# Attention ahead of two expert layers: scaled queries, a negated maximum, and the order of VectorE's step

## The chip, the cores and the metric

One core of a Trainium2 chip runs the whole program. The metric is the device time of one execution in microseconds; "before" is the median of three runs, 1357.63 us (1355.26 to 1357.83). Every profile shown is of one execution.

## The reference, cut to what matters

Two batches, 8 heads, 576 positions, head size 64, all in fp32. A score counts only if it is within tau (0.02) of its row's largest; the rest gets no weight. The attention's output goes through a layer of 8 experts and then one of 4.

```python
scale = 1.0 / np.sqrt(q.shape[-1])                       # 0.125
scores = scale * np.matmul(q, k.transpose(0, 1, 3, 2))
thresh = np.max(scores, axis=-1, keepdims=True) - tau
scores = np.where(scores >= thresh, scores, -1000000000.0)
scores = scores - np.max(scores, axis=-1, keepdims=True)
attn = np.exp(scores)
attn = attn / (np.sum(attn, axis=-1, keepdims=True) + 1e-09)
return np.matmul(attn, v).astype(np.float32)
```

## The kernel before, in words

The program has two parts. In the first, about 250 us, attention runs, and PE does matmuls of the first experts in between (the "fill"). In the second the remaining experts run, with PE busy throughout.

**Units.** Attention is cut into 72 units of 128 query rows against all 576 keys. A unit's scores are two halves of 288 columns in one PSUM tile `sc`, of which there are two. The units come in three groups: 16 "exact" ones (batch 0, queries 0 to 255; weights and values multiplied in plain fp32), 20 (batch 0, the other 320 queries) and 36 (batch 1). Precision beyond fp32r comes from splitting an operand into an fp32r part and the fp32r rest. The first four units (`ws`, the first pair of heads) multiply unsplit queries and keys (L261); the other 68 use queries split by `prep` (L270). A head pair's two leftovers of 64 queries share one unit, whose operands come from `qz`.

**A step.** `step` (L389) issues, in program order, work on up to seven units that stand at different places of the pipeline. Each engine executes its own instructions in that order; semaphores hold an instruction until its inputs are there. With t the step:
- `turn` of unit t-2: PE transposes the normalized weights into `et` (L306), which has one buffer, and `er` (L308).
- `mask` of unit t (VectorE, L288): weights times (score >= threshold), with the row sum as a by-product.
- `top` of unit t+1 (VectorE, L275): the row maximum, read from PSUM.
- `guard` of t (L292), `line` of t+1 (L279: maximum times -0.125, the exponential's bias; L280: the threshold), `norm` of t (L296: reciprocal; L298: GpSimd multiplies the weights by it).
- `hi` of t-2 (ScalarE, L313): the transposed weights as fp32r. `out`: copies of finished products.
- up to three pieces of fill, four matmuls each, and while the exact units run a weight tile split by `cook` (ScalarE cast L96, then GpSimd L98 or VectorE L100).
- `exp` of t+1 (ScalarE, L284): exponential of 0.125 x score + bias, both from per-partition tiles (`esc`, `st`).
- `lo` of t-2 (VectorE, L323, L326): the rest of the transposed weights. The next `turn` needs `et` back from it.
- `scores` of t+2 (PE): needs the buffer that `mask` of t read last.
- deferred subtractions (`later`: L370, L359, L470), the products with the values (L348, L350), more fill, `late` splits.
- work that `plan` (L183) has put at this step for a head that is still to come: keys (`pk`: ScalarE cast L71, GpSimd L76), queries (`pq`: ScalarE cast L239, GpSimd subtraction L240 and, for a leftover, L243), values (`pv`). 22 heads have a `pq`; it comes at least one step ahead of the first scores that use it.

Loads of keys, queries and values go through SP's queue, in order, into two (values: three) buffers, and wait until the split of the tile's former content has read it.

**Scalars.** `on` is 1 if tau is not negative (L527), and then turned into 0 or a huge number (L530); `esc` is 0.125 times it; `lin` holds -0.125 and 8 tau plus `on` (L527 to L531). With unscaled scores the threshold is maximum - 8 tau.

Of the kernel before, what the change touches and what calls it, by code (L numbers as in the profile page):

```python
# [11 lines left out]
AF = mybir.ActivationFunctionType  # L12
ALU = mybir.AluOpType
AX = mybir.AxisListType
# [9 lines left out]
HS = S // 2  # L24
# [5 lines left out]
def attention_two_moe_kernel(ctx, tc, qP, kP, qT, kT, vp, tau, wg, w1, w1s, w2, dp, m2w1s, m2w2, out):  # L30
    nc = tc.nc
    V, A, G, T = nc.vector, nc.scalar, nc.gpsimd, nc.tensor

    def f(ap):
        return ap.bitcast(F32)

    def pool(stack, name, bufs=1, **kw):
        return stack.enter_context(tc.tile_pool(name=name, bufs=bufs, **kw))
# [15 lines left out]
    tau_sb = cp.tile([P, 1], F32, name="tau_sb")  # L54
    warm = cp.tile([P, 1], F32, name="warm")
    A.activation(warm, ones[:, 0:1], AF.Exp)
    esc = cp.tile([P, 1], F32, name="esc")
    lin = cp.tile([P, 2], F32, name="lin")
    on = cp.tile([P, 1], F32, name="on")
# [9 lines left out]
    def split(eh, el, hi, lo, src):  # L69
        if eh is A:  # L70
            A.copy(hi, src)  # L71
        elif eh is V:
            V.tensor_copy(hi, src)
        else:
            G.tensor_scalar(hi, src, 1.0, 1.0, op0=ALU.mult, op1=ALU.mult)
        el.tensor_tensor(lo, src, f(hi), op=ALU.subtract)  # L76
# [34 lines left out]
    class Attention:  # L111
# [117 lines left out]
        def prep(self, hd):  # L229
            pl = self.pl  # L230

            def pk():
                hd["kh"] = pl.tile([P, S], F32R, tag="kh", name="kh", bufs=2)
                hd["kl"] = pl.tile([P, S], F32R, tag="kl", name="kl", bufs=2)
                split(A, G, hd["kh"], hd["kl"], hd["k"])

            def pq():
                qs = hd["qs"] = pl.tile([P, hd["n"]], F32R, tag="qs", name="qs", bufs=2)
                A.copy(qs, hd["q"])  # L239
                G.tensor_tensor(qs[D:], hd["q"][D:], f(qs[D:]), op=ALU.subtract)  # L240
                if hd["rem"]:
                    c, z = hd["rem"]
                    G.tensor_scalar(hd["z"][:, z:z + D], f(qs[:, c:c + D]), 1.0, 1.0, op0=ALU.mult, op1=ALU.mult)  # L243
                self.lq -= 1

            def pv():
                hd["vs"] = pl.tile([P, 5, 2, D], F32R, tag="vhl", name="vhl", bufs=2)
                split(A, G, hd["vs"][:, :, 0, :], hd["vs"][:, :, 1, :], hd["v"])
                self.lv -= 1

            return (pk, pq) if hd["exact"] else (pk, pq, pv)
# [20 lines left out]

        def top(self, u):
            st = u["st"] = self.pl.tile([P, 8], F32, tag="st", name="st", bufs=6)
            V.tensor_reduce(st[:, 0:1], u["sc"][:, :, :HS], axis=AX.XY, op=ALU.max)  # L275

        def line(self, u):
            st = u["st"]
            V.tensor_scalar(st[:, 1:2], st[:, 0:1], lin[:, 0:1], None, op0=ALU.mult)  # L279
            V.tensor_scalar(st[:, 2:3], st[:, 0:1], lin[:, 1:2], None, op0=ALU.subtract)  # L280

        def exp(self, u):
            ex = u["ex"] = self.pl.tile([P, 2, HS], F32, tag="ex", name="ex", bufs=4)
            A.activation(ex, u["sc"][:, :, :HS], AF.Exp, bias=u["st"][:, 1:2], scale=esc)  # L284

        def mask(self, u):
            st, ex = u["st"], u["ex"]
# [101 lines left out]
        def step(self, fill, side):  # L389

            us, t = self.units, self.t
            un = lambda i: us[i] if 0 <= i < len(us) else None
            self.load()
            nxt, a, d, x, c, z, y = (un(t + i) for i in (2, 1, 0, -2, -3, -4, -5))
            if x:
                self.turn(x)
            if d:
                self.mask(d)
            if a:
                self.top(a)  # L400
            if d:
                self.guard(d)
            if a:
                self.line(a)
            if d:
                self.norm(d)
            for part, u in ((2, y), (1, z), (0, c)):
                for g in u["mix"] if u else ():
                    if g["head"]["exact"]:
                        self.mix(g, part)  # L410
            if x:
                self.hi(x)
            for u, late in ((z, False), (y, True)):
                for g in u["mix"] if u else ():
                    if late == (g["head"]["exact"] and g["head"]["h"] < H - 1):
                        self.out(g)
            fill(0, bool(c and c["mix"]))
            if a:
                self.exp(a)
            if x:  # L420
                self.lo(x)
            if nxt:
                self.scores(nxt)
            self.run(self.later)
            for g in c["mix"] if c else ():
                if not g["head"]["exact"]:
                    self.mix(g, 0)
            fill(1, bool(c and c["mix"] or z and z["mix"]))
            self.run(self.late)
            for w in self.work.pop(t, ()):  # L430
                w()
            side()
            self.t += 1
            return self.t < len(us) + 5
# [74 lines left out]
    with ExitStack() as att:  # L509
        ap = pool(att, "attn", side="right")  # L510
        ps_s = pool(att, "ps_s", 2, space=PSUM)
        ps_t = pool(att, "ps_t", 1, space=PSUM)
        ps_r = pool(att, "ps_r", 1, space=PSUM)
        banks.pool = ps = pool(att, "ps_m", 2, space=PSUM)
        at = Attention(ap, ps_s, ps_t, ps_r, ps)
        for p in range(H // 2):
            at.add_pair(0, p, 0, 256, True, p == 0)
        nA0 = len(at.units)
        for p in range(H // 2):
            at.add_pair(0, p, 256, 320, False)  # L520
        nA1 = len(at.units)
        for p in range(H // 2):
            at.add_pair(1, p, 0, S, False)
        at.plan()
        room = [2 * FT]
        at.load()
        V.tensor_scalar(on, tau_sb, 0.0, None, op0=ALU.is_ge)  # L527
        V.tensor_scalar(esc, on, 0.125, None, op0=ALU.mult)
        V.tensor_scalar(lin[:, 0:1], on, -0.125, None, op0=ALU.mult)
        V.tensor_scalar(on, on, -BIG, BIG, op0=ALU.mult, op1=ALU.add)  # L530
        V.scalar_tensor_tensor(lin[:, 1:2], tau_sb, 8.0, on, op0=ALU.mult, op1=ALU.add)  # L531

        def side():
            if at.t >= -1:
                fetch(2)
            if at.t >= nA0 - 3 and raws and room[0] and (at.t < nA1 or room[0] > 2 or at.t % 2):
                room[0] -= 1
                cook()
            if at.t == 20:
                nc.sync.dma_start(wg_sb, wg)  # L540
                nc.sync.dma_start(dp_sb, dp)
            if at.t == 24:
                split(V, V, wg2[:, :, :E1], wg2[:, :, E1:], wg_sb)

        def free(n):
            room[0] += n

        X0, X1 = Expert(0), Expert(1)
        near, far = ((0, 0), (1, P)), ((2, 32), (3, 32 + P))
        todo = [(nA0 + 3, expert_fill(hp, X0, 0, 256, near, acc, None, 0, at.later, keep)),  # L550
                (nA1 + 3, expert_fill(hp, X0, 256, 320, far, acc, tail0[0], 0, at.later, free)),
                (nA1 + 3, expert_fill(hp, X1, 0, 256, near, y1, None, 0, at.later, keep)),
                (nA1 + 3, expert_fill(hp, X1, 256, 320, far, y1, tail0[1], 0, at.later, keep))]

        left, spent = [0], [0]

        def pull(n, end=True):

            for i in range(n):
                if not todo or at.t <= todo[0][0] or (left[0] == 1 and not end):  # L560
                    return i
                left[0] = next(todo[0][1], -1)
                if left[0] < 0:
                    todo.pop(0)
                if left[0] <= 0:
                    left[0] = 0
                    return i + 1
            return n

        def fill(phase, busy):  # L570
            if phase == 0:
                if 0 <= at.t < nA0 - 3:
                    room[0] -= 1
                    cook(None if at.t % 2 else at.later)
                spent[0] = pull(3)
            elif left[0] or not busy:
                pull(max((RA1 if at.t < nA1 + 3 else RA2) - spent[0], 0), True)

        while at.step(fill, side):
            pass  # L580
        at.flush()
        while left[0]:
            pull(1)
        at.flush()
        while raws:
            cook()
            fetch(2)
# [492 lines left out]
```

## Time and profile before

| | |
|---|---|
| median of 3 runs | 1357.63 us (1355.26 to 1357.83) |
| profiled execution: its span, first to last instruction | 1353.7 us |
| profiled execution: its own time | not printed; the three runs lie 1.6 to 4.1 us above the span |
| PE busy | 1320.6 us, 98% |
| VectorE (DVE) busy | 679.6 us, 50% |
| ScalarE (ACT) busy | 562.3 us, 42% |
| GpSimd (POOL) busy | 688.6 us, 51% |
| first and last mask (L288) start | 7.9 and 238.5 us |

Busy shares are means over two very different parts: VectorE is full in attention and half idle behind it. PE's matmuls are pipelined, and a busy PE includes time in which one matmul's end waits; how far PE is from its limit is better read from its waits. "Idle before" and a releaser in brackets say which instruction ended the idle time ahead of an instruction on its engine.

### The profile page before, as it was taken

The page shows a single profiled execution, that of the slowest core. Times are in us where ns is not written, and L with a number is a line of the kernel's source. Part 1 is how long each engine was busy: PE and PEld are TensorE (multiplying, and loading weights), DVE is VectorE, ACT ScalarE, POOL GpSimd, SP SyncE. Part 2 cuts the span into 40 slices and gives each one's busy share as a digit, 9 for nine tenths or more (in the row PEclk, how much of TensorE's full clock was granted, in tenths as well). Part 3 has the DMA queues.
Part 4 walks back from the last instruction along what each step waited for, and adds up shares of the span by engine and source line. Part 5 has one row for each costly group of instructions (what it writes and reads, how often), then busy time and mean ns, then how long its engine had stood idle before and what let it go on. Part 6 is the DMA issues. An engine that isn't in the chain of part 4 may idle for free.

```text
span 1353.7 us, 21670 instructions
## 1 busy us (share of the span) xinstructions
PE 1320.6 (98%) x8089; PEld 1181.8 (87%) x8089; DVE 679.6 (50%) x1600; ACT 562.3 (42%) x1291; POOL 688.6 (51%) x830
## 2 busy tenths in 40 slices
PE   7998999999999999999999999999899999999998
PEld 4588999899888989899898989989789889898987
DVE  6899999365853433434343343434433434343343
ACT  6877777322542423323242332325433334242331
POOL 5866976441774345345434533544963554354330
PEclk9999999999999999999999999999999999999999
DMA  5522330100221111111011111101111101110001
GB/s 173 173 85 72 93 96 26 32 24 24 91 66 39 55 47 40 48 40 62 24 55 47 40 48 40 63 24 56 37 34 55 48 24 56 47 60 27 32 8 63
DMA packets 42058, 73.63 MB, mean 54 GB/s; under 512 B 5088, under 2 KB 10336, under 8 KB 41952
## 3 DMA queue, kind: packets, MB, share of 16 engines
q1 hardware_dynamic: 41664, 71.96, 16.8%
q8 instruction: 64, 1.05, 0.3%
q14 instruction: 42, 0.34, 0.1%
q10 hardware_dynamic: 288, 0.28, 0.1%
HBM read 69.86 MB, written 2.36 MB: 53 GB/s over the span
## 4 chain that ended last, share of the span: by engine, by line
PE 83%; DVE 8%; POOL 4%; ACT 3%; issue 2%; DMA 1%; POOLq 0%; ACTq 0%; DVEq 0%
PE mm L997 37%; PE mm L887 32%; PE mm L489 5%; PE mm L461 3%; DVE ex L288 2%; DVE st L275 1%; PE sc L270 1%; PE et L306 1%; ACT ex L284 1%; PE pv L350 1%; PE pv L341 1%; PE pv L348 1%; POOL wl L76 1%; DVE etl L323 1%; DVE xy L772 0%
## 5 line engine op out<-in xcount | busy, mean ns | idle before, releaser
L997 PE MATMUL mm<-wh,hs 128*128 128x512 f32 x1344 | 436.7, 398 | 3.7 <-DVE hs L863 3.7
L76 POOL TENSOR_TENSOR wl<-raw,wh 128x512 fp32r<-128x512 f32 x154 | 199.1, 1304 | 328.4 <-ACT wh L71 326.5
L997 PEld LDWEIGHTS mm<-wh,hs 128*128 128x128 f32 x1344 | 253.0, 188 | 66.3 <-DVE hs L863 10.1
L1005 DVE SCALAR_TENSOR_TENSOR acc<-mm,p,acc 128x512 f32<-128x512 f32 x181 | 135.9, 751 | 308.1 <-PE mm L997 308.1
L997 PE MATMUL mm<-wl,hs 128*128 128x512 f32 x672 | 264.7, 394 | 0.0
L892 ACT COPY s<-mm 128x288 f32<-128x288 f32 x84 | 33.6, 401 | 453.5 <-PE mm L887 453.5
L863 DVE SCALAR_TENSOR_TENSOR hs<-mm,hs 128x288 fp32r<-128x288 f32 x252 | 114.8, 456 | 104.0 <-ACT hs L862 103.7
L997 PEld LDWEIGHTS mm<-wl,hs 128*128 128x128 f32 x672 | 127.0, 189 | 27.3
L887 PE MATMUL mm<-xh,wl 128*128 128x288 f32 x672 | 144.3, 296 | 2.6 <-ACT w L892 1.4
L887 PE MATMUL mm<-xl,wh 128*128 128x288 f32 x672 | 143.8, 295 | 0.0
L887 PE MATMUL mm<-xh,wh 128*128 128x288 f32 x672 | 143.8, 295 | 0.0
L862 ACT ACTIVATE hs<-mm 128x288 fp32r<-128x288 f32 x252 | 104.2, 414 | 71.8 <-DVE mm L914 66.6
L76 POOL TENSOR_TENSOR wl<-ws,wh 128x512 fp32r<-128x512 f32 x88 | 114.5, 1305 | 36.6 <-ACT wh L71 26.9
L887 PEld LDWEIGHTS mm<-xh,wl 128*128 128x128 f32 x672 | 110.0, 188 | 7.3 <-ACT w L892 1.9
L887 PEld LDWEIGHTS mm<-xh,wh 128*128 128x128 f32 x672 | 108.1, 188 | 0.0
L887 PE MATMUL mm<-xth,wl 128*128 128x288 f32 x504 | 107.9, 295 | 0.0
L887 PEld LDWEIGHTS mm<-xl,wh 128*128 128x128 f32 x672 | 107.9, 188 | 0.0
L887 PE MATMUL mm<-xth,wh 128*128 128x288 f32 x504 | 107.7, 295 | 0.0
L887 PE MATMUL mm<-xtl,wh 128*128 128x288 f32 x504 | 107.7, 295 | 0.0
L869 POOL TENSOR_SCALAR ht<-hs 128x128 fp32r<-128x128 f32 x168 | 49.2, 298 | 112.9 <-ACT hs L862 97.8
L71 ACT CAST wh<-raw 128x512 fp32r<-128x512 f32 x154 | 95.7, 624 | 13.3 <-PE mm L887 10.4
L625 POOL TENSOR_TENSOR ws<-raw 128x512 f32<-128x512 f32 x44 | 57.7, 1311 | 54.6 <-DMA raw<-in_w1s 32.5
(169 smaller groups left out, 2412.0 us busy)
## 6 DMA issues: line engine op xcount, KB each, us to landing
raw<-in_w SPq DMA_DIRECT2D x88, 256.0 KB, 3.0
raw<-in_w1s SPq DMA_DIRECT2D x56, 256.0 KB, 2.8
raw<-in_m2w1s SPq DMA_DIRECT2D x32, 256.0 KB, 2.7
raw<-in_m2w SPq DMA_DIRECT2D x32, 256.0 KB, 2.8
kr<-in_kT SPq DMA_DIRECT2D x22, 288.0 KB, 2.9
vr<-in_vp SPq DMA_DIRECT2D x24, 160.0 KB, 2.3
qr<-in_qT SPq DMA_DIRECT2D x8, 288.0 KB, 2.8
out_y<-acc SPq DMA_DIRECT2D x8, 256.0 KB, 2.0
```

The source lines that it names most:

```text
L71: A.copy(hi, src)
L76: el.tensor_tensor(lo, src, f(hi), op=ALU.subtract)
L461: T.matmul(ph[:, :n], lhsT=a[:, kt * P:(kt + 1) * P], rhs=x[:, kt, n0:n0 + n], start=i == 0 and kt == 0, stop=i == 2 and kt == KT - 1)
L489: T.matmul(py[:, :256], lhsT=x, rhs=a[:, c0:c0 + 256], start=i == 0, stop=i == 3 * FT - 1)
L625: G.tensor_tensor(s, a, b, op=op)
L862: A.activation(hh, src, AF.Relu)
L863: V.scalar_tensor_tensor(hl, src, 0.0, f(hh), op0=ALU.max, op1=ALU.subtract)
L869: G.tensor_scalar(tail[j][:, :, q:q + 32], f(side[s][j][:, :, 2 * P:]), 1.0, 1.0, op0=ALU.mult, op1=ALU.mult)
L887: T.matmul(m, lhsT=w[:, (2 * g + kt) * P:(2 * g + kt + 1) * P], rhs=operand(u, kt, lo), start=first and j == 0, stop=j == len(ops) - 1, sk ...
L892: A.copy(z[name], m)
L997: T.matmul(py, lhsT=hs[x][:, k, o:o + P], rhs=w, start=n == 0, stop=n == 3 * HF - 1)
L1005: V.scalar_tensor_tensor(acc[t], py, s, acc[t], op0=ALU.mult, op1=ALU.add)
```

## The change

Four edits, all in attention:
- `pq` multiplies the queries by `esc` in place, with a ScalarE activation (Copy with a scale from a tile), ahead of the cast. The scores of 68 units are then already scaled.
- `top` writes the negated maximum for these units, `exp` takes it as its bias directly and has no scale tile; the four unsplit units keep the old form.
- `line` is one instruction for these units: maximum - (tau + `on`), formed from the negated maximum; `on` gets tau added once at the start.
- In the step, VectorE's order becomes maximum (t+1), mask (t), line (t+1), guard (t), reciprocal (t); it was mask, maximum, guard, line, reciprocal.

```diff
             def pq():
                 qs = hd["qs"] = pl.tile([P, hd["n"]], F32R, tag="qs", name="qs", bufs=2)
+                A.activation(hd["q"], hd["q"], AF.Copy, scale=esc)
                 A.copy(qs, hd["q"])
                 G.tensor_tensor(qs[D:], hd["q"][D:], f(qs[D:]), op=ALU.subtract)
...
         def top(self, u):
             st = u["st"] = self.pl.tile([P, 8], F32, tag="st", name="st", bufs=6)
-            V.tensor_reduce(st[:, 0:1], u["sc"][:, :, :HS], axis=AX.XY, op=ALU.max)
+            V.tensor_reduce(st[:, 0:1], u["sc"][:, :, :HS], axis=AX.XY, op=ALU.max, negate=not u["q"][0][0]["ws"])
 
         def line(self, u):
             st = u["st"]
+            if not u["q"][0][0]["ws"]:
+                V.tensor_scalar(st[:, 2:3], st[:, 0:1], -1.0, on, op0=ALU.mult, op1=ALU.subtract)
+                return
             V.tensor_scalar(st[:, 1:2], st[:, 0:1], lin[:, 0:1], None, op0=ALU.mult)
             V.tensor_scalar(st[:, 2:3], st[:, 0:1], lin[:, 1:2], None, op0=ALU.subtract)
 
         def exp(self, u):
             ex = u["ex"] = self.pl.tile([P, 2, HS], F32, tag="ex", name="ex", bufs=4)
-            A.activation(ex, u["sc"][:, :, :HS], AF.Exp, bias=u["st"][:, 1:2], scale=esc)
+            if u["q"][0][0]["ws"]:
+                A.activation(ex, u["sc"][:, :, :HS], AF.Exp, bias=u["st"][:, 1:2], scale=esc)
+            else:
+                A.activation(ex, u["sc"][:, :, :HS], AF.Exp, bias=u["st"][:, 0:1])
...
             if x:
                 self.turn(x)
+            if a:
+                self.top(a)
             if d:
                 self.mask(d)
             if a:
-                self.top(a)
+                self.line(a)
             if d:
                 self.guard(d)
-            if a:
-                self.line(a)
-            if d:
                 self.norm(d)
...
         V.scalar_tensor_tensor(lin[:, 1:2], tau_sb, 8.0, on, op0=ALU.mult, op1=ALU.add)
+        V.tensor_tensor(on, tau_sb, on, op=ALU.add)
```

## Rows read from the trace of the kernel before

**Rows 1.** The head of the page.
```profile
span 1353.7 us, 21670 instructions
```

**Rows 2.** Stretches: busy us of PE, PEld, DVE, ACT, POOL; granted clock, DMA share, GB/s.
```profile
31.94:66.00 34.06, 32.13 (x169) 19.11 (x167) 27.17 (x92) 28.10 (x54) 29.66 (x32) 1.00 0.58 173
66.00:120.84 54.84, 51.33 (x404) 49.41 (x403) 51.22 (x156) 39.63 (x79) 34.69 (x43) 1.00 0.28 83
120.84:180.39 59.55, 55.09 (x410) 52.29 (x409) 55.62 (x168) 44.77 (x86) 48.90 (x79) 1.00 0.29 90
180.39:239.50 59.11, 57.59 (x462) 56.00 (x461) 55.16 (x171) 44.54 (x87) 39.18 (x43) 1.00 0.16 48
```

**Rows 3.** Chain that ended last, in order of time: start us, us, what.
```profile
27.02 0.73 PE sc L270 x4
...
39.10 0.84 ACT ex L284
39.96 0.82 DVE ex L288 x2
40.78 0.67 DVE st L275
```

**Rows 4.** Waits (us, times, longest): VectorE 5-66, 66-240; PE 66-240 (two); PE 5-66.
```profile
DVE ex L288 <- ACT ex L284: 10.0, 13, 1.7
...
DVE ex L288 <- ACT ex L284: 5.0, 18, 0.6
...
PE et L306 <- DVE etl L323: 6.3, 9, 1.0
PE sc L270 <- DVE ex L288: 2.0, 3, 1.0
...
PE sc L270 <- POOL qs L240: 2.8, 2, 2.4
```

**Rows 5.** Groups by form, 0 to 250 us: busy us, mean ns, idle before.
```profile
L284 ACT ACTIVATE ex<-sc,st,esc 128x576 f32<-128x576 f32 x72 | 59.9, 832 | 16.5 <-DVE st L279 14.5 <-POOL ex L298 0.5 <-POOL wl L98 0.5
...
L275 DVE TENSOR_REDUCE st<-sc 128x1 f32<-128x576 f32 x72 | 54.2, 752 | 0.8 <-PE sc L261 0.8
...
L279 DVE TENSOR_SCALAR st<-st,lin 128x1 f32<-128x1 f32 x72 | 15.4, 214 | 0.0
...
L280 DVE TENSOR_SCALAR st<-st,lin 128x1 f32<-128x1 f32 x72 | 14.7, 204 | 0.0
```

**Rows 6.** Timeline of VectorE's small instructions in one step: start us, us, instruction.
```profile
88.66 0.14 DVE L292 TENSOR_SCALAR st<-st 128x1 f32<-128x1 f32 x1
88.78 0.21 DVE L279 TENSOR_SCALAR st<-st,lin 128x1 f32<-128x1 f32 x1
88.91 0.20 DVE L280 TENSOR_SCALAR st<-st,lin 128x1 f32<-128x1 f32 x1
```

**Rows 7.** Timeline of the first units, 0 to 34 us.
```profile
3.49 4.35 PE L261 MATMUL sc<-kr,qr 64*128 64x288 f32 x8 [3.49 <-DMA qr<-in_qP]
...
5.96 0.76 DVE L275 TENSOR_REDUCE st<-sc 128x1 f32<-128x576 f32 x1 [0.79 <-PE sc L261]
...
8.91 2.25 PE L261 MATMUL sc<-kr,qr 64*128 64x288 f32 x4 [1.06 <-DVE ex L288]
...
15.51 0.85 PE L270 MATMUL sc<-kh,qs 128*128 128x288 f32 x2 [0.39 <-POOL qs L240]
...
16.16 0.68 PE L270 MATMUL sc<-kl,qs 128*128 128x288 f32 x2
...
18.85 0.74 POOL L298 TENSOR_SCALAR ex<-ex,st 128x576 f32<-128x576 f32 x1 [2.55 <-DVE st L296]
...
23.06 0.54 PE L270 MATMUL sc<-kh,qs 128*128 128x288 f32 x2 [2.38 <-POOL qs L240]
```

**Rows 8.** The query cast's line: duration ns min/median/max, first and last start.
```profile
L239 ACT CAST qs<-qr x22: 392/458/679, 13.2 to 216.5; 128x320 fp32r<-128x320 f32 x8, 128x576 fp32r<-128x576 f32 x8, 128x256 fp32r<-128x256 f32 x6
```

**Rows 9.** L270's idle time before its matmuls and weight loads, by releaser: us, times.
```profile
  DVE ex L288: 9.8, 15
```

## The prediction

> **What bounds the kernel now.** I read the span first [rows 1], then the attention part in stretches [rows 2], because the diff touches nothing after it. Behind about 250 us the order of the instructions stays as it is and PE is the engine that is always busy, so a microsecond won or lost in attention should show whole at the end. The three runs have a median of 1357.63 us. The profiled execution has a span of 1353.7 us; its own time is not printed beside it, so 3.9 us stand around the span if it was a median run and 1.6 us if it was the fastest (1355.26). I work out a difference from its rows and set it against the median.
>
> In the stretches behind 66 us VectorE is 93% busy (51.22 + 55.62 + 55.16 of 173.5 us), ScalarE 74%, GpSimd 71%. PE reads 95%, but its spans are modelled, and what it idles is better seen in its waits. A step there takes about 3.3 us ((239.5 - 66) / 53 units). In the stretch before, 31.94 to 66, no engine is full: DVE 80%, ACT 83%, POOL 87%. There the chain of waits goes round a ring [rows 3]: exponential 0.84, mask 0.82, maximum 0.67 us, then the guard and the first threshold instruction, and the next exponential. With 0.12 + 0.21 us for these two and small handoffs it is 2.7 us, one unit per round, each waiting for the one before.
>
> The waits say the same [rows 4]: the mask waited for the exponential 10.0 us in 13 places up to 66 us and 5.0 us in 18 places behind it. PE's longest wait behind 66 us is 6.3 us in nine places, for the low halves that VectorE subtracts last in a step (L323). So late in attention VectorE's time is the limit in some steps, PE's own work in the others.
>
> **The change, part by part.**
> *One small instruction less.* For 68 of the 72 units (all but the four on unsplit scores) L279 disappears; L280 becomes an instruction with two scalar operands of the same size, priced the same, 0.204 us. L279 lasts 0.214 us [rows 5], but the next starts 0.13 us after it [rows 6], so VectorE wins 0.13 a unit: 68 x 0.13 = 8.8 us of busy time, 6.9 of them behind 66 us (53 units). The exponential's bias is now the maximum itself, which takes guard and L279 out of the ring too.
> *Negation inside the reduction.* No row shows it. Nothing excludes a cost up to one small instruction, 0.14 us by the guard of rows 6, and nothing suggests a gain. I take 0.752 us as before; the upper end is 72 x 0.14 = 10 us. The single extra addition at the start (as small) lies before the first maximum, where VectorE waits for scores anyway.
> *Order: maximum, mask, threshold, guard, reciprocal.* The maximum no longer queues behind a mask that waits for an exponential, so the ring is cut: VectorE reduces the next unit while ScalarE exponentiates. What replaces it is another loop. There are two score buffers; the mask of unit t frees the one for the scores of t+2, and the maximum of t+2 now stands in front of the mask of t+1. So the new ring is mask 0.82, scores 0.73 (rows 3, at 27.02), maximum 0.67 to 0.75, and handoffs: 2.4 us. In the middle stretch that is 0.3 us a unit for some 12 units, 3.6 us. POOL's 29.66 of 34.06 us caps it at 4.4, so I take 2.5; the ends are 0 and 4.4. Moved with it are only VectorE instructions: no DMA is issued there and no queue of SP or POOL is passed. But the reciprocal comes a maximum later (0.67 us), and POOL's normalization with it. PE transposes that unit two steps later, so about three microseconds cover it; without that cover PE would lose up to 0.67 a unit.
> *Behind 66 us* the offer is 6.9 us of small instructions and 5.0 of mask waits. PE can only take what it stalls, and the part that hangs on VectorE is 6.3 + 2.0 us in rows 4. I take 6.0; the ends are 0, if PE's own work fills the steps, and 8.3.
> *The start, where the new ring costs.* Scores of the first units are slow [rows 7]: 2.25 us a unit for L261, 1.33 for the first L270 (15.51 to 16.84). Walk: maximum 1 at 7.9, mask 0 to 9.4, scores 2 to 11.8, maximum 2 to 12.6, mask 1 to 13.4, scores 3 to 15.7, maximum 3 to 16.5, mask 2 to 17.3, scores 4 to 18.7, maximum 4 to 19.5, mask 3 to 20.3, normalization 3 at 20.7. Before it was 18.85, and POOL had waited 2.55 us for it, so POOL starts its full stretch 1.9 us late, and the scores at 23.06, which wait for POOL's split of the queries, come that much later: +1.9 us.
> *The queries scaled in place.* 22 more ScalarE instructions stand ahead of the cast that L239 does. No row shows a Copy with a pointer scale. From below it is the cast of the same tile, 0.392 to 0.679 us, median 0.458 [rows 8], 22 x some 0.5 = 11 us; from above the exponential, 0.832 with two pointer operands on the widest tile [rows 5], 1.24 times as much, 14 us. I take the cast, since both are plain passes from SBUF. ScalarE idles a quarter of the late stretches, and the split is made a step or more before its scores, so this lies beside other work but for two places where PE waited for POOL's share (2.8 us in rows 4, two times): 2 x 0.4 = 0.8 us. If the cover is gone it is the full 11 to 14.
> *The exponential without a scale operand.* It lies between 0.832 (as now) and the widest cast, 0.679. I take 0.832; at the other end ScalarE wins 68 x 0.15 = 10 us, nearly all of it idle time.
> The Trainium skill, "ScalarE: Activation LUTs", section "What ACT_TABLE_LOAD costs", says that each pointer operand of an ACTIVATE adds about 93 ns. That speaks against the scaled copy (22 x 0.093 = 2.0 us more) and for the exponential (68 x 0.093 = 6.3 us less); no row of this trace has the same tile with one and with two, and by the page the sum would be about 1 us better, 0.093 for each of some dozen units of the middle stretch.
>
> **Sum:** -2.5 - 6.0 + 1.9 + 0.8 = -5.8, taken as -5.6: 1357.6 - 5.6 = **1352.0 us**.
>
> **Rivals.**
> *PE is the bound.* PE would be late by its own work in nearly all steps behind 66 us, VectorE's waits would move elsewhere, and only 2.5 of the middle would stand against 2.7 of start and copies: 1357.8, no change. For it: PE 95% busy, 57.59 of 59.11 in the last stretch. Against: nine stalls for VectorE of 0.7 us each.
> *The score buffer becomes the wait (slower).* PE waited for a mask in 15 places, 9.8 us in sum, before the scores of L270 [rows 9]. If each mask comes a maximum later, each of these grows by 0.67: 10 us, and with the start 1.9 it is 11.9 against 8.8 of instructions saved: +3.1, 1360.7 us. It decides if PE's added wait is over 0.13 us a unit on average, which is what the dropped instruction brings. Against it: in the late steps PE has fill matmuls ahead of the scores, and the maximum starts earlier than before.
> *All stalls go.* The middle gives 4.4, behind 66 us all 8.3 go, the scaled copies are hidden and the start costs 0.7: -12.0, 1345.6 us.
> That the change does not do what it says (a bias that still waits for the threshold instruction) would show in the waits and give the PE-bound time.
>
> **Numbers.** Forecast 0.55 (own range 1347 to 1355), PE bound 0.20, score buffer 0.13, all stalls gone 0.12. A measurement of this kernel tells about 0.2% from no change (2.7 us). Faster is 0.55 + 0.12 = 0.67, same 0.20, slower 0.13. The range leaves out about half of the fastest and half of the slowest case: 1345 to 1360.5.
>
> **What would show it.** Right: the mask's wait for the exponential falls from 15 us to under 3; L279 has 4 instances; the chain of 31.94 to 66 has no three-piece ring; stalls for L323 fall from 6.3 us to about 2; POOL's normalization 3 comes near 20.7; total VectorE busy time falls by about 9 us. Wrong: the maximum waits for scores, or the scores for the mask, in most steps; POOL's query split is waited for in more than a few places; or attention ends earlier but what follows gives it back, which my sum excludes.

## The result, and the profile after

The changed kernel takes 1363.4 us (1362.74 to 1365.22, four runs), 1.0057 of the kernel before, 95% interval 1.0045 to 1.0069: 7.7 us slower, where 5.6 us less were forecast. The time lies outside the range, on the other side. The two medians as printed, 1363.4 and 1357.63, are only 5.8 us apart, because the kernel before was run just three times here (a fourth execution of it took 2225.16 us and is left out); 79 later runs of it, in the four sessions of the experiments, have medians of 1355.6 to 1355.93, 7.5 to 7.8 below the changed kernel. Executions of one kernel differ with the TensorE clock that they were granted, as a mean share of full speed: those 79 took 1353.9 to 1355.0 us at 0.999 and 1357.8 to 1358.9 us at 0.995. The changed kernel's profiled execution has a span of 1361.7 us, 8.0 more than before [rows 1].

It was lost in attention. The row of the mask's line, with the first and last start at its end, says so for the kernel after:

```profile
L295 DVE SCALAR_TENSOR_TENSOR ex<-sc,st,ex x72: 798/807/819, 8.7 to 247.7; 128x576 f32<-128x576 f32 x72
```

The last mask started at 238.5 us before; it is 9.2 us later now. What follows it takes 1.2 us less in these two executions, which is less than executions of one kernel differ by. The chain of waits of the kernel after shows what stands there now (start us, us, what; its longest pieces), first in the stretch that answers to rows 3, then in two later places:

```profile
39.70 0.74 DVE ex L295 x2
40.49 0.80 PE sc L271 x4
41.83 0.59 PE pv L348 x2
43.29 0.63 ACT wh L96
43.94 0.98 DVE wl L100
44.92 0.67 DVE st L276
45.59 0.74 DVE ex L295 x2
46.38 0.80 PE sc L271 x4
...
94.02 0.66 DVE st L276
94.69 0.74 DVE ex L295 x2
95.47 1.33 PE sc L271 x8
...
149.16 0.73 ACT ex L291
149.90 0.67 ACT qr L239
150.59 0.68 ACT qs L240
```

The exponential is gone from the ring: maximum, mask and scores now follow one another, with no gap but the handoff (94.02 + 0.66, 94.69 + 0.74, 95.47). Scores hold 13.1% of the chain up to 262 us (L271), where they held 6.9% of it up to 260 us before (L270). In the exact stretch the chain goes on through PE's products behind the scores, a ScalarE cast and a VectorE subtraction before it comes to the next maximum: PE executes in order, so whatever stands behind blocked scores is late too (the scores end at 41.29, the products behind them start at 41.83). The last three lines are a scaled copy and a cast in the chain, 1.35 us together.

The waits of the kernel after (us in sum, times, longest), VectorE and PE up to 68 us, then VectorE and PE behind it, with the lines that answer to rows 4:

```profile
DVE st L276 <- PE sc L271: 7.2, 11, 1.8
DVE st L276 <- PE sc L262: 4.8, 4, 1.9
...
PE sc L262 <- DVE st L283: 3.4, 2, 1.7
PE sc L271 <- DVE ex L295: 2.9, 6, 0.7
...
DVE etl L330 <- ACT eth L320: 11.3, 23, 1.2
DVE st L276 <- PE sc L271: 4.1, 9, 1.4
...
PE et L313 <- DVE etl L330: 5.4, 10, 1.0
PE sc L271 <- DVE st L281: 3.3, 4, 1.6
PE sc L271 <- DVE ex L295: 1.4, 2, 1.2
```

The mask no longer waits for an exponential: that part of the change did what it says. In its place the maximum waits for scores, 16.1 us in 24 places, and the low halves (L330) wait 11.3 us for their high halves from ScalarE. PE's scores wait for a mask, or for the threshold instruction just behind it, 11.4 us in 15 places from 0 to 250 us, where it was 5.3 us in 8 places. What the new instructions cost, by form (busy us, mean ns, idle before):

```profile
L276 DVE TENSOR_REDUCE st<-sc 128x1 f32<-128x576 f32 x72 | 54.2, 753 | 16.9 <-PE sc L271 11.2 <-PE sc L262 4.8
L291 ACT ACTIVATE ex<-sc,st 128x576 f32<-128x576 f32 x68 | 50.3, 740 | 0.7 <-DVE st L276 0.3
...
L239 ACT ACTIVATE qr<-qr,esc 128x576 f32<-128x576 f32 x8 | 6.2, 774 | 0.0
...
L240 ACT CAST qs<-qr 128x576 fp32r<-128x576 f32 x8 | 5.4, 674 | 0.3
```

The negation is free (753 ns, 752 in rows 5), and the exponential without a scale operand is 92 ns shorter (740, against 832 in rows 5).

### The profile page after: what moved, and what is told of

Its sections match the earlier page's. It is cut to its first block, busy times and chain, and to the rows that moved or that the text cites. A ratio compares the mean times of both kernels' runs of the same rounds, so it can differ in the third digit from the quotient of the medians.

```text
span 1361.7 us, 21482 instructions
## 1 busy us (share of the span) xinstructions
PE 1321.3 (97%) x8089; PEld 1182.4 (87%) x8089; DVE 674.6 (50%) x1533; ACT 568.4 (42%) x1313; POOL 688.6 (51%) x830
## 4 chain that ended last, share of the span: by engine, by line
PE 86%; DVE 8%; ACT 3%; POOL 2%; issue 1%; DMA 0%; POOLq 0%; ACTq 0%; DVEq 0%
PE mm L1004 37%; PE mm L894 32%; PE mm L495 5%; PE mm L467 3%; PE sc L271 3%; DVE ex L295 1%; PE et L313 1%; DVE st L276 1%; PE pv L357 1%; PE pv L348 1%; PE pv L355 1%; DVE etl L330 1%; PE sc L262 1%; DVE xy L779 1%; POOL wl L76 0%
## 5 line engine op out<-in xcount | busy, mean ns | idle before, releaser
L71 ACT CAST wh<-raw 128x512 fp32r<-128x512 f32 x154 | 95.7, 624 | 13.7 <-PE mm L894 10.4
```

## The experiments

Each ratio is to the kernel before, measured on the same chip in the same session, with its 95% interval.

**The order alone.** Only VectorE's order is changed.
```diff
+            if a:
+                self.top(a)
             if d:
                 self.mask(d)
             if a:
-                self.top(a)
+                self.line(a)
             if d:
                 self.guard(d)
-            if a:
-                self.line(a)
-            if d:
                 self.norm(d)
```


> VectorE's order alone (maximum, mask, line, guard, reciprocal); queries unscaled, two threshold instructions, bias from L279. Theory A (the score buffers: the mask that frees a buffer now stands behind the maximum, so scores, maximum and mask form a ring that PE waits in): slower than before by 6 to 11 us, near 1365, since the start costs 1.9 us and the exponential now also waits for the mask and one threshold instruction; PE idles for L288 before the scores, and the maximum for scores, in most steps up to 66 us. Rival B (the scaled copies on ScalarE cost the time, the order gains): faster than before, 1352 to 1355. Rival C (only both together lose): within 2 us of before.

Measured: 1365.46 us, 1.0067 (1.0053 to 1.0081), +9.1 us. The order does not gain by itself; it costs about what the whole change does (the two intervals overlap). Theory A stands, B and C fall. The chain of this kernel has the ring bare (start us, us, what):

```profile
36.41 0.80 PE sc L270 x4
37.20 0.02 issue
37.23 0.76 DVE st L275
37.99 0.73 DVE ex L288 x2
```

**The scaling alone.** The change without its new order (VectorE's lines as before).
```diff
+                A.activation(hd["q"], hd["q"], AF.Copy, scale=esc)
                 A.copy(qs, hd["q"])
...
+                A.activation(ex, u["sc"][:, :, :HS], AF.Exp, bias=u["st"][:, 0:1])
```


> Scaled queries, negated maximum and one threshold instruction, with VectorE's old order. Theory A: faster than before by 3 to 6 us, 1352 to 1355: the ring exponential, mask, maximum falls from 2.70 us to about 2.4 (bias straight from the maximum, exponential 0.73 us and not 0.83), and mask waits for the exponential shrink. Rival B: the 22 copies cost it, 1360 to 1364. Rival C: within 2 us of before.

Measured: 1356.59 us, 1.0005 (0.9995 to 1.0015): no difference. So the order costs 1.0057 - 1.0005 = 0.52%, 7.0 us, on top of the scaled queries, with the two intervals together some 2 us wide either way. The expected gain did not come, and the next run says where some of it went. From 66 to 245 us VectorE's longest wait is now another one, so time that its instructions save is waited for again; first the kernel before, then this one:

```profile
DVE etl L323 <- ACT eth L313: 4.7, 8, 1.4
```
```profile
DVE etl L330 <- ACT eth L320: 10.4, 18, 1.9
```

**The copies alone.** The kernel before, with the in-place copy by a tile of ones.
```diff
+                A.activation(hd["q"], hd["q"], AF.Copy, scale=ones[:, 0:1])
                 A.copy(qs, hd["q"])
```


> The kernel before with one more in-place ScalarE Copy of the queries, scaled by a tile of ones, so that its values stay as they are: the price of the copies alone. Theory A: +1 to +2 us (in the chain of the changed kernel such a copy stands in three places, 0.67 us each), 1358.5 to 1360. Rival B: +5 us and more, most of what the change lost.

Measured: 1360.03 us, 1.0026 (1.0016 to 1.0037), +3.5 us, between the two expectations and about twice theory A's. If costs and gains simply add up, then with the scaling's 1.0005 the short threshold, the direct bias and the shorter exponential win some 2.8 us (0.7 - 3.5), and the copies take them back; each of the two numbers is uncertain by over 1 us.

**The old order for the first four steps.** The whole change, but VectorE keeps its old order while the first units' slow scores run.
```diff
-            if a:
+            if a and t >= 4:
                 self.top(a)
             if d:
                 self.mask(d)
+            if a and t < 4:
+                self.top(a)
...
```


> The whole change, but steps before step 4 keep VectorE's old order, so that the first units' slow scores don't stand in the new ring. Theory A: 1.5 to 2 us faster than the changed kernel, 1361.5, with normalization 3 back near 18.9 us. If the start is absorbed later, no difference: 1363.

Measured: 1361.31 us, 1.0041 (1.0028 to 1.0054), 2.1 us better than the whole change by the two ratios, as theory A had it. The two intervals overlap, but the trace bears it out. Normalization 3 is back where it was before [rows 7], at 18.85 us; this is GpSimd's timeline of this kernel, and below it the kernel after:

```profile
18.85 0.74 POOL L305 TENSOR_SCALAR ex<-ex,st 128x576 f32<-128x576 f32 x1 [2.42 <-DVE st L303]
```
```profile
13.55 2.25 PE L262 MATMUL sc<-kr,qr 64*128 64x288 f32 x4 [1.68 <-DVE st L283]
...
15.84 0.76 DVE L276 TENSOR_REDUCE st<-sc 128x1 f32<-128x576 f32 x1 [1.93 <-PE sc L262]
16.52 0.81 DVE L295 SCALAR_TENSOR_TENSOR ex<-sc,st,ex 128x576 f32<-128x576 f32 x1
...
20.79 0.74 POOL L305 TENSOR_SCALAR ex<-ex,st 128x576 f32<-128x576 f32 x1 [1.53 <-DVE st L303]
```

PE's scores wait for VectorE (1.68), the maximum for the scores (1.93), the mask for the maximum, and GpSimd for all of it. The scores read nothing that L283 writes, so I read a wait for L283 as one for the mask just ahead of it on VectorE.

**The ring cut, first try.** The mask compares the weights with exp(-tau), so the exponential frees the score buffer; once with the old and once with the new order, both with scaled queries.
```diff
+        A.activation(warm, tau_sb, AF.Exp, scale=-1.0)
...
-            V.scalar_tensor_tensor(ex, u["sc"][:, :, :HS], st[:, 2:3], ex, op0=ALU.is_ge, op1=ALU.mult,
+            V.scalar_tensor_tensor(ex, ex, warm[:, 0:1], ex, op0=ALU.is_ge, op1=ALU.mult,
```


> Scaled queries, old order, and the mask compares the weights with exp(-tau) and not the scores with the threshold, so that it does not read the score buffer any more: the exponential is what frees it. Both theories: near the scaled kernel with the old order, 1352 to 1358; it is the base for the next one. The mask's own length may change (both inputs from SBUF), 0.67 to 0.82 us.

> The same mask with the new order. Theory A (the score buffer's ring costs the time): with the ring cut, the order loses at most 2 us against the old order with the same mask, and may gain; PE's wait for L295 ahead of the scores is gone. Rival D (it is the later mask, reciprocal and normalization themselves, which the transposes wait for): still 5 to 8 us slower than the old order with the same mask.

Measured: 1369.47 us, 1.0101 (1.0084 to 1.0117) with the old order, 1375.79 us, 1.0145 (1.0129 to 1.0161) with the new. The base was spoiled: the mask with two inputs from SBUF is longer in the mean, and no longer of one length (by form, old order, with GpSimd's normalization beside it):

```profile
L295 DVE SCALAR_TENSOR_TENSOR ex<-ex,warm 128x576 f32<-128x576 f32 x72 | 73.2, 1017 | 13.1 <-ACT ex L291 10.2 <-ACT ex L289 1.8
L305 POOL TENSOR_SCALAR ex<-ex,st 128x576 f32<-128x576 f32 x71 | 62.6, 882 | 30.7 <-DVE st L303 27.7 <-PE sc L271 2.7
```

With the new order its mean is 1130 ns, 113 more than with the old, 8.1 us over 72 masks, so the 6 us between the two say nothing on the ring. Inconclusive.

**The ring cut, second try.** The mask reads the scores of the next unit, so it no longer keeps the right weights. Instruction and memories stay the same; only the buffer that it holds differs.
```diff
+            sc = self.units[min(self.t + 1, len(self.units) - 1)]["sc"]
-            V.scalar_tensor_tensor(ex, u["sc"][:, :, :HS], st[:, 2:3], ex, op0=ALU.is_ge, op1=ALU.mult,
+            V.scalar_tensor_tensor(ex, sc[:, :, :HS], st[:, 2:3], ex, op0=ALU.is_ge, op1=ALU.mult,
```


> Scaled queries, old order; the mask of a unit compares the scores of the next unit (already there, same shape, also in PSUM) and not its own, so that its own score buffer is free once the exponential and the mask before it are done. What it computes differs; its instructions and their lengths don't. Both theories: within 3 us of the scaled kernel with the old order, 1353 to 1358; it is the base for the next one.

> The same mask with the new order. Theory A (scores, maximum and mask in a ring through the two score buffers): with the ring cut, the new order costs at most 2 us against the old order with the same mask, where it costs 7 with the ring, and the first units are no longer 1.9 us late. Rival D (the later mask, reciprocal and normalization cost it): 5 us or more against the old order with the same mask.

Measured: 1355.22 us, 0.9989 (0.998 to 0.9998) with the old order, 1356.72 us, 1.0004 (0.9995 to 1.0013) with the new. The order now costs 0.15%, 2.0 us, and not 7.0. The plainest comparison is with the whole change, from which the second kernel differs in the mask's buffer alone: 1.0057 falls to 1.0004, 7.2 us. The old order is not quite a clean base here, since its mask now needs the next unit's scores and waits for them 4.1 us in 5 places. The mask keeps its length:

```profile
L296 DVE SCALAR_TENSOR_TENSOR ex<-sc,st,ex x72: 800/808/820, 8.6 to 237.8; 128x576 f32<-128x576 f32 x72
```

The last mask starts at 237.8 us, 9.9 before that of the changed kernel. With the new order and the ring cut, no wait of PE's scores for a mask or a threshold is left, and the maximum's wait for scores is 8.4 us and not 16.1 (VectorE up to 68 us, then behind it):

```profile
DVE st L276 <- PE sc L271: 4.4, 7, 1.7
...
DVE st L276 <- PE sc L262: 2.0, 3, 0.8
...
DVE st L276 <- PE sc L271: 2.0, 6, 0.4
```

Theory A stands for some 5 of the 7 us. What the remaining 2 are was not settled: rival D, the later normalization, may hold them, but not the 7, and the runs with the new order were granted a little less clock (a mean of 0.996, against 0.997).

**Where the copies stand.** Scaled queries with the old order, and the copy issued with the key split, a step or so ahead of the cast; then the same place, but by GpSimd; then the first only for the heads that are not exact, with the exact ones as in the change.
```diff
                 split(A, G, hd["kh"], hd["kl"], hd["k"])
+                A.activation(hd["q"], hd["q"], AF.Copy, scale=esc)
...
-                A.activation(hd["q"], hd["q"], AF.Copy, scale=esc)
                 A.copy(qs, hd["q"])
```


> The scaled queries with VectorE's old order, but the in-place copy issued with the head's key split, ahead of the cast's step for most heads. Theory A1 (a copy costs where it stands right ahead of the next step's transposed weights on ScalarE, together with the cast): the +3.5 us of the copies shrink to 1 to 2, so 1.5 to 2.5 us faster than the same kernel with the copy at the cast, about 0.998 of before. Rival (any 11 us more on ScalarE cost the same wherever they stand): no difference to that kernel, 1.0005 of before.

Measured: 1355.17 us, 0.9989 (0.9979 to 0.9999). A little better than at the cast, less than hoped; the intervals of the two overlap.

```diff
+                G.tensor_scalar(hd["q"], hd["q"], esc, 1.0, op0=ALU.mult, op1=ALU.mult)
```


> As the last one, but the scaling is done by GpSimd, in place, behind the key split. Theory A1: ScalarE is relieved of the copies, so up to 3.5 us faster than the scaled kernel with the old order, 0.997 of before, if GpSimd's 22 x 0.4 to 0.8 us are hidden; in the stretch from 32 to 66 us, where GpSimd is 87% busy, up to 2 us may come back. Rival (the dependence of the split on one more instruction costs, not ScalarE's time): 1.0005 of before or slower.

Measured: 1356.49 us, 1.0004 (0.9995 to 1.0013). ScalarE is free of the copies, and nothing is won: the rival's number. Whether GpSimd's own time took it or the longer way to the cast, this run does not tell.

```diff
                 split(A, G, hd["kh"], hd["kl"], hd["k"])
+                if not hd["exact"]:
+                    A.activation(hd["q"], hd["q"], AF.Copy, scale=esc)
...
+                if hd["exact"]:
+                    A.activation(hd["q"], hd["q"], AF.Copy, scale=esc)
                 A.copy(qs, hd["q"])
```


> Scaled queries, old order; the in-place copy stands ahead of the cast for the exact heads and with the key split for the others. Theory A1 (it matters where the copies stand): from the two traces, the early copies lost 1.2 us up to 66 us and won 1.7 behind it, so this takes the better of both: 1 us faster than the early copies, 0.998 of before. Rival: no difference to the early copies, 0.999.

Measured: 1351.0 us, 0.9968 (0.9955 to 0.998): 4.3 us faster than the kernel before. That it beats the early copies is not shown: its runs were granted a clock of 0.996 to 0.999 and nine of their twelve 0.995, and at 0.998 the two kernels took 1350.77 and 1350.93 us. Its span is 1349.0 us and its last mask starts at 235.0, 3.5 us earlier than before. The old ring is still in its chain, but shorter:

```profile
38.57 0.75 ACT ex L294
39.32 0.03 issue
39.35 0.82 DVE ex L298 x2
40.17 0.67 DVE st L279
40.84 0.06 DVE st L302
```

**The exact heads alone.** The last kernel with only its six split exact heads scaled; all others as before, without copies.
```diff
-            if u["q"][0][0]["ws"]:
+            if u["q"][0][0]["ws"] or not u["q"][0][0]["exact"]:
                 A.activation(ex, u["sc"][:, :, :HS], AF.Exp, bias=u["st"][:, 1:2], scale=esc)
...
-                if not hd["exact"]:
-                    A.activation(hd["q"], hd["q"], AF.Copy, scale=esc)
```


> Scaled queries, negated maximum and one threshold instruction for the six split exact heads alone (12 units); all others as before; old order; no copies for the other 16 heads. If what the last kernel won (0.9968) was all won in the stretch up to 66 us, where the ring exponential, mask, maximum stood: 0.997 to 0.998. If the part behind 66 us with its copies moved ahead wins on its own: about 0.999, only the 1.5 us that the scaled kernel stood ahead at 62 us.

Measured: 1354.38 us, 0.9997 (0.9987 to 1.0008). So what the mixed kernel wins, it wins mostly behind 66 us, with the copies ahead of the cast's step, and not in the exact stretch; the first of the two expectations falls.

## Why the prediction was wrong, step by step

Where each term came out can be read from the starts of the masks (us, one profiled execution each; "ring cut" is the second try with the new order):

| | before | after | order alone | scaling alone | ring cut |
|---|---|---|---|---|---|
| mask of unit 4 | 19.86 | 21.89 | 22.42 | 19.81 | 19.68 |
| mask of unit 16 | 57.36 | 59.28 | 61.53 | 56.34 | 56.47 |
| last mask | 238.46 | 247.68 | 248.78 | 237.75 | 237.83 |

The changed kernel is 2.0 us late at unit 4, 1.9 at unit 16 and 9.2 at the last mask. So the start cost what was forecast, the middle gave nothing where -2.5 was taken, and the rest of attention lost 7.3 us where -6.0 and a share of the copies' 0.8 were taken.

**The step that failed first** is the new ring, "mask 0.82, scores 0.73, maximum 0.67 to 0.75, and handoffs: 2.4 us", taken as a gain of 0.3 us a unit against a ring of 2.7, "one unit per round". Its length was right: in the chain of the order alone, from the start of the scores to the end of the mask behind them it is 2.31 us (36.41 to 38.72). But only every second round is of this kind. Three masks in a row, before and then after:

```profile
33.90 0.82 DVE L288 SCALAR_TENSOR_TENSOR ex<-sc,st,ex 128x576 f32<-128x576 f32 x1 [0.77 <-ACT ex L284]
37.26 0.82 DVE L288 SCALAR_TENSOR_TENSOR ex<-sc,st,ex 128x576 f32<-128x576 f32 x1
39.96 0.82 DVE L288 SCALAR_TENSOR_TENSOR ex<-sc,st,ex 128x576 f32<-128x576 f32 x1 [0.77 <-ACT ex L284]
```
```profile
36.00 0.81 DVE L295 SCALAR_TENSOR_TENSOR ex<-sc,st,ex 128x576 f32<-128x576 f32 x1
39.62 0.81 DVE L295 SCALAR_TENSOR_TENSOR ex<-sc,st,ex 128x576 f32<-128x576 f32 x1
42.00 0.81 DVE L295 SCALAR_TENSOR_TENSOR ex<-sc,st,ex 128x576 f32<-128x576 f32 x1
```

The short round went from 2.70 to 2.38 us, as forecast; the other went from 3.36 to 3.62, and two rounds together still take 6.0. In that other round VectorE also subtracts a weight tile (L100), and the chain of the kernel after comes to it through the scores, PE's products and ScalarE's casts (40.49 to 44.92 above). The old ring runs through ScalarE and VectorE; the new one runs through PE's in-order queue, and what stands behind blocked scores pays. With the ring cut two rounds take 5.7 to 6.0 us as well, so the middle did not hang on this ring alone.

**The term behind 66 us, "-6.0", failed** by more. The sum has no price for the new ring there, where a step of 3.3 us is longer than the ring's 2.4. From unit 16 to the last mask the kernel before takes 181.1 us, the changed one 188.4 and the order alone 187.3; with the buffer freed in another way, the same order takes 181.4. So the score buffer is what costs, here above all. The direct waits do not add up to it: those of scores for a mask or threshold behind 68 us are 4.7 us, against 2.0 before. The rest is argued from PE's order and not taken apart piece by piece; what fits it is that ScalarE's wait for the transposes ahead of the high halves (0 to 250 us) is 27.0 us, where it is 20.0 before and 19.2 with the ring cut.

The gain that was to come did not come with the old order either: the scaled kernel gains nothing in total. I read nine waits for L323 as VectorE being late, and counted what VectorE would save. But L323 itself waits for ScalarE's high halves, and through them for PE's transposes and the single `et` buffer. When VectorE was relieved, its wait for them grew, from 4.7 us before to 10.4 in the scaled kernel (both from 66 to 245 us), and to 11.3 in the changed one; PE's wait for these low halves, which was to fall from 6.3 us to about 2, is 5.4. A stall that ends with an engine's instruction is no measure of that engine's load; one has to ask what this instruction waited for.

**The start, +1.9, was right** in size and in mechanism: normalization 3 was walked out to 20.7 us and came at 20.79, and the old order in the first four steps returns 2.1 us by the two ratios.

**The copies, +0.8, were mis-sized**: they cost 3.5 us, between the 0.8 taken and the 11 to 14 named for lost cover. That ScalarE idles a quarter of the time was not enough cover: the copy stands in its queue ahead of the query cast and of the next step's high halves, and is in the chain in three places, as at 149.9 us. Moving most of the copies a step ahead turned +0.7 us into -4.3, with more clock granted to the second kernel (0.998, against 0.997); moving all of them gave -1.5, with less (0.996). That the place of the copies matters is likely by these runs; how much it is worth, and why the same copies on GpSimd win nothing, stays open.

**The threshold and the bias** did what was said, and the negation is free; but VectorE's busy time fell by 5.0 us (679.6 to 674.6) and not by 9. The Trainium skill's figure in "ScalarE: Activation LUTs", "What ACT_TABLE_LOAD costs", 93 ns for each pointer operand, agrees with both rows: the exponential lost 92 ns with its scale operand, and the scaled copy is 100 ns longer than the cast of the same tile (774 and 674). I had taken the cast for the copy; that is 2 us of ScalarE time. The terms add up to -5.8, so the sum's 1352.0 should read 1351.8, and 0.832 is 1.23 times 0.679, not 1.24; neither matters.

**The rivals.** "The score buffer becomes the wait" is what happened, priced 1360.7 with a chance of 0.13. That its price came near is partly luck. The 15 waits of [rows 9] count weight loads (9 times, 6.0 us) and matmuls (6 times, 3.8 us) of the same scores apart, and the two overlap on PE, so the growth by 0.67 each was counted too often; on the other side it left out what stands behind PE's queue. Its argument against itself, that in the late steps fill matmuls stand ahead of the scores, was no protection: the scores at 95.47 start right behind the mask. The chance should have been larger, because the old profile already had waits of just this kind before anything was put in front of the mask.

## What to carry to other kernels

When an instruction is moved ahead of another on one engine, look at which buffer the other one frees, and follow that buffer to the next user and back: with two buffers, putting the reader of the new one in front of the reader of the old one closes a ring through the producer, and everything behind the producer in its in-order queue pays. A saved instruction is worth what the next wait lets through, so ask of each stall what the instruction that ends it was itself waiting for. An instruction that is added to an engine with idle time can still cost: look at what stands behind it in the queue, and try it a step ahead. And before a ring is set against another, look at several rounds: here every second one went another way.

## What the runs showed of the hardware

With both inputs from SBUF the mask took 1017 ns in the mean, a quarter more than with one from PSUM (815 before), and single ones far longer; GpSimd's normalization grew with it, from a mean of 771 ns to 882. The row of the mask's line, minimum, median and maximum in ns:

```profile
L295 DVE SCALAR_TENSOR_TENSOR ex<-ex,warm x72: 802/916/1965, 8.4 to 252.2; 128x576 f32<-128x576 f32 x72
```

The two inputs alone cost nothing that these rows show. Of these 72 masks, 8 ran with no GpSimd instruction beside them, by the profile's spans, and took 802 to 821 ns; the other 64 took 1042 ns in the mean. In the kernel before, with one input from PSUM, 66 of 72 had GpSimd at work beside them and took 814 ns in the mean. With the longer masks the whole kernel lost 13 us against the scaled one (1.0101 to 1.0005), more than any other edit here. The Trainium skill, "GPSIMD Engine Reference", section "Key points", says that GpSimd shares its SBUF interfaces with VectorE and contends with VectorE instructions that have two SBUF inputs; the runs agree, and give it a size.
